# The odd middle rows of a transform: one fp32 product over 64 partitions instead of two fp32r products over 128

## The chip, the core and the metric

The kernel runs on one core of a Trainium2 chip. The metric is the device time of one execution in microseconds (us), given as the median of several runs; less is better. The engines are named as in the profile: PE is TensorE's matrix product, PEld its weight load, DVE is VectorE, ACT ScalarE, POOL GpSimd and SP the engine that issues most transfers.

## What is computed

A two-dimensional Fourier transform of eight batches of 3072 x 256 numbers, of which the real part is kept, and then a feed-forward layer with a parametric ReLU on each of the 24576 rows.

```python
X = np.fft.fft(x, axis=1)
X = np.fft.fft(X, axis=2)
x = X.real.astype(np.float32).reshape(B * S, D)      # 24576 x 256
h = x @ w_in                                         # 256 -> 2048
g = np.maximum(h, 0.0) + alpha * np.minimum(h, 0.0)
return (g @ w_out).astype(np.float32)                # 2048 -> 256
```

## The kernel before

**The feed-forward stream.** The transform along the 256 features is folded into `w_in`. What is left is the transform along the 3072 positions, batch by batch, whose result stands in the tile `X`, and the two products of the layer. They run as one stream of steps. A step takes one block of output columns (386, 384 or 512 wide) and one sixteenth of the 2048 hidden units. `ffn1` makes its two halves of the hidden product in six fp32r matmuls (`pq`, lines 755 to 757), `pair` makes sums and the ReLU of them (`d`, `pq`; DVE at 781 and 728, ACT at 785), `split_parts` cuts each into a high and a low part (`hi` on ACT at 734, `lo` on POOL at 736), and `ffn2` multiplies these with `woh` and `wol` in twelve matmuls (line 854). A step works three steps ahead on `ffn1`. The first batch has 64 steps, the six in the middle 48 each, the last 64.

**The transforms beside it.** While the steps of batch b run, batch b + 1 is folded (line 415, on POOL and DVE) and transformed. A batch has eight transforms, each one call of `dft` (line 557): the four even ones, `see`, `cee`, `ceo` and `seo`, one in each of four steps that the table `UNITS` names, between the fourth and the last pair of `ffn2`'s product groups; and two odd ones, `ca` and `sb`, for the cosine part `co` and two for the sine part `so`, in the first and the fourth step of the next batch (`unit_odd`). A transform writes one PSUM bank `ps`, which is one of the four banks that `ffn1` uses too. The order on every engine is the order of the program; there is no scheduler.

**The middle rows.** The folded rows are kept in tiles of 128 partitions, and a transform needs sums over rows with an odd index, of which 32 lie on partitions 96 to 127 of one tile and 32 on partitions 64 to 95 of another. Where `middle` holds nothing for a batch (the first two), `dft` makes the odd sum out of three fp32 matmuls of 192 to 194 columns. From the third batch on, `mids` first gathers these 64 rows: ACT writes their high part (fp32r) to partitions 64 to 127 of a tile (line 600), POOL the low part to partitions 0 to 63 (line 601). The odd sum is then two fp32r matmuls over 128 partitions, one with the high part of the table (`mh`) and one with its low part (`ml`), and one fp32 matmul. `parts_table` cuts the six tables so at six steps of the second batch. The calls `mids("se")` and `mids("ce")` stand at step 37 of a middle batch, `mids("co")` and `mids("so")` at steps 44 and 46, each of these two behind `turn_rows`, in which ACT scales six pieces (line 486) and POOL adds them (lines 488 and 489). At the end of a block, `evacuate` copies `acc` out of PSUM, half on ACT (line 891) and half on DVE.

**In the trace.** An fp32 matmul shows as two matmul records and two weight loads, an fp32r matmul as one of each. A record's shape begins with the part of the array that it uses, as rows times columns: 128\*128 everywhere, but 128\*8 in two early transforms of one feature column (tile `f`), which have 8 output partitions.

Of the kernel before, what the change touches and what calls it, by code (L numbers as in the profile page):

```python
# [9 lines left out]
F32 = mybir.dt.float32  # L10
# [80 lines left out]
def _tables():  # L91
    p = PI.reshape(3, P)
    j, i2 = J1[None, :], J2[None, :]

    def five(full, whole=False):

        n = full.shape[-1]
        at = np.concatenate([np.arange(97), [0]]) if n == 193 else np.arange(96)
        full = np.concatenate([full, np.zeros((3, P, n % 2))], 2)
        r = p[:, :, None] % 4  # L100
        if whole:
            at = np.arange(n)
        parts = [full[0][:, at] * (r[0] == 0), full[0] * (r[0] % 2), full[1][:, at] * (r[1] == 2), full[1] * (r[1] % 2)]
        return np.concatenate(parts + [full[2]], 1)

    def both(full):

        n = full.shape[-1] // 2 * 2 + full.shape[-1] % 2 * 2
        v = np.zeros((P, 194))
        rows = np.concatenate([full[1][ROW[1]], full[0][ROW[0]]])  # L110
        two = np.zeros((64, n))
        two[:, :full.shape[-1]] = rows
        v[:, :n] = np.concatenate([two, two])[:, np.arange(n).reshape(n // 2, 2).T.reshape(-1)]
        return v

    turn, q = _cos(p, 3072), p[:, :, None]
    s = _sin(q * (2 * i2 + 1), 1536)
    s[0][0] = _sin(384 * (2 * i2 + 1), 1536)[0]
    made = dict(
        cee=_cos(q * j, 768), see=_sin(q * j, 768), ceo=_cos(q * (2 * i2 + 1), 1536), seo=s,  # L120
        ca=turn[:, :, None] * _cos(q * j, 768), sb=turn[:, :, None] * _sin(q * j, 768),
    )
    m, d = np.arange(D)[:, None], np.arange(P)[None, :]
    feat = np.stack([_cos(m * d, D), _sin(m * d, D)], 1)
    feat[:, 1, 0] = (-1.0) ** np.arange(D)
    feat = feat.reshape(2, P, 2, P).transpose(1, 0, 2, 3)
    ident = np.stack([np.eye(P), -np.eye(P)], 1)
    out = dict(
        ee=np.stack([five(made["cee"]), five(made["see"])], 1), eo=np.stack([five(made["ceo"]), five(made["seo"])], 1),
        er=np.concatenate([five(made["ca"], True), five(made["sb"])], 1), mids=np.stack([both(v) for v in made.values()], 1),  # L130
        feat=feat, ident=ident,
    )
    return {k: np.ascontiguousarray(v, dtype=np.float32) for k, v in out.items()}
# [19 lines left out]
def fft2_prelu_ffn(ctx: ExitStack, tc: tile.TileContext, t, outputs):  # L153
# [367 lines left out]
    TABS = dict(cee=ee[:, 0], see=ee[:, 1], ceo=eo[:, 0], seo=eo[:, 1], ca=er[:, 0:968], sb=er[:, 968:])  # L521
    middle = {}

    def parts_table(kind):

        n, v = list(TABS).index(kind), []
        for h in "hl":
            v.append(late.tile([P, 194], F32R, tag=f"m{kind}{h}", name="m" + h))
        S.activation(out=v[0], in_=raw_mids[:, n], func=ACTF.Copy)
        G.tensor_tensor(out=v[1], in0=raw_mids[:, n], in1=v[0].bitcast(F32), op=ALU.subtract)  # L530
        middle[kind] = v

    def dft(kind, v, zr, m, mid=None, bank=None):

        ps = (bank or other_bank())[0:m]
        tab = TABS[kind]
        w, o = {778: (98, 194), 768: (96, 192), 968: (193, 194)}[tab.shape[-1]]
        col = np.cumsum([0, w, o, w, o, o])
        t_ = [tab[:, a:b] for a, b in zip(col, col[1:])]
        first, second = [(v[:, 0], t_[0])], [(v[:, 1], t_[2])]  # L540
        if zr is not None:
            r = res[:, 98:98 + 193 + (mid is not None)] if w == 193 else res[:, 0:w]
            if mid is not None:
                first.insert(0, (zr, r))
            else:
                first.append((zr.bitcast(F32), r.bitcast(F32)))
        if mid is None:
            odd = [(v[:, 0], t_[1]), (v[:, 2], t_[4]), (v[:, 1], t_[3])]
        else:
            odd = [(mid, _halves(u[:, 0:o])) for u in middle[kind]] + [(v[:, 2], t_[4])]  # L550
        sums = [(0, first), (OAT, odd), (w, second)]
        if w == 193:
            sums = [(0, first + second), (OAT, odd)]
        for at, terms in sums:
            for i, (lhsT, rhs) in enumerate(terms):
                out = ps[:, at:at + int(np.prod(rhs.shape[1:]))]
                nc.tensor.matmul(  # L557
                    out=_pairs(out) if len(rhs.shape) > 2 else out, lhsT=lhsT, rhs=rhs,
                    start=(i == 0), stop=(i == len(terms) - 1),
                )  # L560
        return ps, 192 if o == 192 else 193, m, kind
# [30 lines left out]

    def mids(b, nm):

        two = middle[nm] = late.tile([P, 2, P], F32R, tag=f"m{nm[0]}", name="m" + nm)
        v, o = fold[b, nm, "all"], 3 if nm[1] == "o" else 0
        for c in range(2):
            r = ROW[c]
            hi, lo, v2 = two[r], two[r.start - 64:r.stop - 64], v[r, o + c:o + c + 4:3]
            S.activation(out=hi, in_=v2, func=ACTF.Copy)  # L600
            G.tensor_tensor(out=lo, in0=v2, in1=hi.bitcast(F32), op=ALU.subtract)

    def mid_of(nm, i):
        return middle[nm][:, i] if nm in middle else None

    def unit_odd(b, nm):

# [289 lines left out]
    LEAD = 3  # L897
    AHEAD = 4
    SPLITS = {9: (6, 7), 10: (8, 9), 11: (10, 11), 12: (12, 13), 13: (0, 1), 14: (2, 3), 15: (4, 5)}
    TABLE_STEPS = (7, 11, 18, 22, 26, 30)  # L900
    UNITS = {53: "see", 55: "cee", 57: "ceo", 58: "seo"}, {39: "see", 40: "cee", 41: "ceo", 42: "seo"}
    FOLDS = ((0, G, 0, 0.25), (1, G, 0.25, 0.5), (3, G, 0.5, 0.75), (4, G, 0.75, 1), (2, V, 0, 0.5), (5, V, 0.5, 1))

    def step(s, between=None):
# [120 lines left out]
    for b in range(NB):  # L1025
        mine = [g for g, block in enumerate(BLOCKS) if block[0] == b]
        r_odd, r_fold, r_end = (16, 16, 50) if b == 0 else (0, 4, 36)
        beside = []
        for r in range(len(mine) * KF):
            s = mine[0] * KF + r  # L1030
            g, f = divmod(s, KF)
            kind = (UNITS[b > 0]).get(r) if b + 1 < NB else None
            if kind is None:
                step(s)
            else:
                bank = lambda: unit_mm(b + 1, kind, pq.tile([P, 512], F32, tag="pq", name="ps"))
                unit(b + 1, kind, G, step(s, bank))
            if b == 0:
                if r == 3:
                    nc.sync.dma_start(out=er, in_=t["er"])  # L1040
                if r == 9:
                    column_128_store("ceo", butterfly(*column_128_mm("ceo")))
                if r in (10, 11):
                    unit(0, ("ceo", "seo")[r - 10], G)
                if r in (12, 13):
                    if r == 13:
                        fold_128(0)
                    turn_rows(0, ("co", "so")[r - 12])
                if r == 25:
                    start.close()  # L1050
                    late = ctx.enter_context(tc.tile_pool(name="late", bufs=1))
                    raw_mids = late.tile([P, 6, 194], F32, tag="raw", name="raw_mids")
                    nc.sync.dma_start(out=raw_mids, in_=t["mids"])
            if b == 1 and r in TABLE_STEPS:
                parts_table(list(TABS)[TABLE_STEPS.index(r)])
            if f == 10:
                load_xbc(g + 1)
            q = r - r_odd
            if q in (0, 3):
                unit_odd(b, ("co", "so")[q // 3])  # L1060
            if b + 1 < NB:
                if r == r_fold:
                    fold_tiles(b + 1)
                for i, e, r0, r1 in FOLDS:
                    r0, r1 = (r_fold + round(v * (r_end - r_fold)) for v in (r0, r1))
                    if r == r0:
                        by = one_by_one if e is V else spread
                        beside.append(by(fold_whole(6 * b + 6 + i, e), r0, r1))
                for x in beside:
                    next(x, None)  # L1070
                if r == r_end + 1:
                    fold_rows(b + 1)
                    fold_128(b + 1)
                for nm, at in zip(("se", "ce", "co", "so"), (51, 52, 60, 62) if b == 0 else (37, 37, 44, 46)):
                    if r == at:
                        if nm[1] == "o":
                            turn_rows(b + 1, nm)
                        if b:
                            mids(b + 1, nm)


_INS = [
# [61 lines left out]
```

## Time and profile before

| | |
|---|---|
| median of 3 runs | 1671.02 us (1669.03 to 1671.09) |
| profiled execution | 1671.85 us, of which 1670.1 us are the span from the first to the last instruction |
| granted clock of TensorE, mean | 0.998 of full |
| busy | PE 98%, PEld 87%, DVE 91%, ACT 68%, POOL 80% |
| chain that ended last | PE 80%, DVE 8%, POOL 5%, ACT 4% |

The span and 1.75 us around it make up the profiled execution, which is 0.8 us over the median. A matmul's listed duration is from its start until its last result is out; the next one starts before that, so what a matmul costs is the distance from its start to the next start.

### The profile page before, as it was taken

To read this page: it belongs to the slowest core of one execution; us is meant where nothing else is said; L and a number is where in the kernel's file an instruction comes from. 1 tells how busy PE (TensorE), PEld (TensorE's weight loads), DVE (VectorE), ACT (ScalarE), POOL (GpSimd) and SP (SyncE) were. 2 spreads that over 40 slices of the span, in tenths; PEclk is the share of its full clock that TensorE was granted. 3 is DMA by queue.
4 is the path that set the end of the run, shared out by engine and by line. 5 is a ranking of instruction groups with operands and counts; after the bars stand their busy time and mean duration, and the time that the engine had idled before them with its cause. 6 is when DMAs were issued, how large, how long until landed. Compare 5 with 4: busy or idle time off the path is not lost.

```text
span 1670.1 us, 26532 instructions
## 1 busy us (share of the span) xinstructions
PE 1639.2 (98%) x8240; PEld 1458.9 (87%) x8240; DVE 1518.1 (91%) x2708; ACT 1130.5 (68%) x2092; POOL 1341.1 (80%) x1439
## 2 busy tenths in 40 slices
PE   8989999999999999999999999999999999999998
PEld 7779999888888888888888888888888888889998
DVE  7979998999889998899989998899988999889997
ACT  5865667666676666766676666766667666677765
POOL 2378987899888887889888898888887888776666
PEclk9999999999999999999999999999999999999999
DMA  6410120011000110000100101001110010000000
GB/s 234 140 58 33 45 69 20 8 70 39 32 26 20 57 52 20 32 39 32 70 1 32 51 33 58 26 7 70 39 32 26 20 45 31 1 31 25 25 20 20
DMA packets 25403, 70.48 MB, mean 42 GB/s; under 512 B 5718, under 2 KB 7726, under 8 KB 25262
## 3 DMA queue, kind: packets, MB, share of 16 engines
q1 hardware_dynamic: 23918, 68.27, 11.5%
q8 instruction: 66, 1.08, 0.3%
q10 hardware_dynamic: 1344, 0.52, 0.1%
q14 instruction: 75, 0.61, 0.1%
HBM read 43.50 MB, written 25.26 MB: 41 GB/s over the span
## 4 chain that ended last, share of the span: by engine, by line
PE 80%; DVE 8%; POOL 5%; ACT 4%; issue 2%; DMA 1%; DVEq 0%; ACTq 0%; POOLq 0%; SPq 0%
PE acc L854 49%; PE pq L755 9%; PE pq L756 8%; PE pq L757 8%; PE ps L557 3%; DVE d L781 2%; POOL lo L736 2%; DVE d L728 2%; PE acc L824 2%; DVE pf L773 1%; ACT pq L785 1%; ACT hi L734 1%; DVE y L590 1%; DMA feat<-in_feat 1%; PE ps L351 1%
## 5 line engine op out<-in xcount | busy, mean ns | idle before, releaser
L736 POOL TENSOR_TENSOR lo<-d,hi 128x512 fp32r<-128x512 f32 (+2 forms) x804 | 971.6, 1225 | 228.5 <-ACT hi L734 205.9
L734 ACT ACTIVATE hi<-d 128x512 fp32r<-128x512 f32 (+2 forms) x804 | 482.1, 600 | 352.3 <-DVE d L728 250.0
L728 DVE SCALAR_TENSOR_TENSOR d<-d,sg,pq 128x512 f32<-128x512 f32 (+2 forms) x804 | 565.0, 703 | 22.0 <-ACT pq L785 22.0
L785 ACT ACTIVATE pq<-d,sga 128x512 f32<-128x512 f32 (+2 forms) x804 | 525.9, 655 | 54.0 <-DVE d L781 53.6
L781 DVE TENSOR_TENSOR d<-pf,pq 128x512 f32<-128x512 f32 (+2 forms) x832 | 530.4, 641 | 20.6 <-POOL lo L736 11.8
L854 PE MATMUL acc<-hi,woh 128*128 128x512 f32 (+2 forms) x1604 | 456.1, 365 | 6.4 <-ACT o L891 6.4
L854 PE MATMUL acc<-lo,woh 128*128 128x512 f32 (+2 forms) x1604 | 394.3, 366 | 0.0
L854 PE MATMUL acc<-hi,wol 128*128 128x512 f32 (+2 forms) x1604 | 392.6, 365 | 0.0
L773 DVE SCALAR_TENSOR_TENSOR pf<-xbc,w,pq 128x512 f32<-128x512 f32 (+2 forms) x416 | 298.5, 718 | 67.9 <-PE pq L757 60.5
L854 PEld LDWEIGHTS acc<-hi,woh 128*128 128x128 f32 x1604 | 297.9, 189 | 41.3 <-ACT o L891 10.5
L755 PE MATMUL pq<-X,wih 128*128 128x512 f32 (+2 forms) x832 | 310.8, 374 | 15.7 <-DVE d L728 12.2
L854 PEld LDWEIGHTS acc<-hi,wol 128*128 128x128 f32 x1604 | 295.2, 189 | 30.7
L854 PEld LDWEIGHTS acc<-lo,woh 128*128 128x128 f32 x1604 | 292.6, 189 | 29.5
L756 PE MATMUL pq<-X,wih 128*128 128x512 f32 (+2 forms) x832 | 302.5, 364 | 0.3 <-DVE X L661 0.3
L757 PE MATMUL pq<-X,wil 128*128 128x512 f32 (+2 forms) x832 | 302.4, 363 | 0.0
L755 PEld LDWEIGHTS pq<-X,wih 128*128 128x128 f32 x832 | 157.2, 189 | 48.5 <-PE pq L757 12.0
L757 PEld LDWEIGHTS pq<-X,wil 128*128 128x128 f32 x832 | 157.6, 189 | 15.5
L756 PEld LDWEIGHTS pq<-X,wih 128*128 128x128 f32 x832 | 157.7, 190 | 14.5 <-issue 0.5
L415 POOL TENSOR_TENSOR raw<-raw 128x512 f32<-128x512 f32 (+2 forms) x84 | 69.5, 827 | 0.0
L320 POOL TENSOR_TENSOR w<-we,wm 128x512 int32<-128x512 int32 x16 | 20.4, 1272 | 44.4 <-DVE wm L311 43.3
L891 ACT ACTIVATE o<-acc 128x512 f32<-128x512 f32 (+2 forms) x50 | 25.6, 563 | 22.4 <-PE acc L854 22.2
L661 POOL TENSOR_TENSOR X<-yo,X 128x384 fp32r<-128x384 f32 x32 | 31.1, 993 | 11.2 <-ACT X L660 11.2
(184 smaller groups left out, 1099.2 us busy)
## 6 DMA issues: line engine op xcount, KB each, us to landing
raw<-in_xh SPq DMA_DIRECT2D x46, 512.0 KB
out<-o SPq DMA_DIRECT2D x36, 512.0 KB
raw<-in_w SPq DMA_DIRECT2D x15, 512.0 KB
xbc<-xcd SPq DMA_DIRECT2D x18, 256.0 KB
out<-o SPq DMA_DIRECT2D x8, 386.0 KB
out<-o SPq DMA_DIRECT2D x6, 384.0 KB
before<-in_xh SPq DMA_DIRECT2D x2, 512.0 KB
xbc<-xcd SPq DMA_DIRECT2D x5, 193.0 KB
```

The lines of the kernel that those rows point to most:

```text
L415: yield size, lambda o=o, i0=i0, i1=i1, op=op: e.tensor_tensor(out=o, in0=i0, in1=i1, op=op)
L557: nc.tensor.matmul(out=_pairs(out) if len(rhs.shape) > 2 else out, lhsT=lhsT, rhs=rhs, start=(i == 0), stop=(i == len(terms) - 1),)
L728: V.scalar_tensor_tensor(out=g, in0=d, scalar=sg[:, f:f + 1], in1=ad, op0=ALU.mult, op1=ALU.max)
L734: S.activation(out=hi, in_=d, func=ACTF.Copy)
L736: G.tensor_tensor(out=lo, in0=d, in1=hi.bitcast(F32), op=ALU.subtract)
L755: nc.tensor.matmul(out=out, lhsT=wih[:, f, q], rhs=xh, start=True, stop=False)
L756: nc.tensor.matmul(out=out, lhsT=wih[:, f, q], rhs=xl, start=False, stop=False)
L757: nc.tensor.matmul(out=out, lhsT=wil[:, f, q], rhs=xh, start=False, stop=True)
L773: V.scalar_tensor_tensor(out=_pairs(pf), in0=_halves(xbc[g]), scalar=w128[:, f:f + 1], in1=_pairs(ps[0]), op0=ALU.mult, op1=ALU.add,)
L781: V.tensor_tensor(out=d, in0=pf, in1=ps[1], op=ALU.add if i else ALU.subtract)
L785: S.activation(out=ad, in_=d, func=ACTF.Copy, scale=sga[:, f:f + 1])
L854: nc.tensor.matmul(out=out, lhsT=wt[:, f, o * P:(o + 1) * P], rhs=rhs, start=(f == 0 and n[o] == 0), stop=(f == KF - 1 and n[o] == 2),)
```

## The change

Six things change.

- `mids` copies the 64 rows once, in fp32, to partitions 64 to 127. The two subtractions on POOL are gone.
- The odd sum's two fp32r products become one fp32 product whose two operands lie on partitions 64 to 127 alone.
- `parts_table` with its six ACT copies and six POOL subtractions is gone; the table is loaded to 64 partitions and used as it is.
- The second batch, too, gets gathered rows: its `mids` calls run at steps 51, 52, 60 and 62 of the first batch. Its transforms have two fp32 products in the odd sum instead of three.
- With that, the small product with `zres` in `cee` and `ca` of the second batch is fp32r instead of fp32, as it was from the third batch on.
- `see` and `cee` move from steps 39 and 40 to steps 38 and 39.

```diff
     def both(full):
-        n = full.shape[-1] // 2 * 2 + full.shape[-1] % 2 * 2
-        v = np.zeros((P, 194))
...
+        v = np.zeros((64, 194))
+        v[:, :full.shape[-1]] = np.concatenate([full[1][ROW[1]], full[0][ROW[0]]])
...
-            odd = [(mid, _halves(u[:, 0:o])) for u in middle[kind]] + [(v[:, 2], t_[4])]
+            odd = [(mid, mids_of[64:, list(TABS).index(kind), 0:o]), (v[:, 2], t_[4])]
...
-        two = middle[nm] = late.tile([P, 2, P], F32R, tag=f"m{nm[0]}", name="m" + nm)
+        two = middle[nm] = late.tile([P, 2, P], F32, tag=f"m{nm[0]}", name="m" + nm)
         v, o = fold[b, nm, "all"], 3 if nm[1] == "o" else 0
         for c in range(2):
-            r = ROW[c]
-            hi, lo, v2 = two[r], two[r.start - 64:r.stop - 64], v[r, o + c:o + c + 4:3]
-            S.activation(out=hi, in_=v2, func=ACTF.Copy)
-            G.tensor_tensor(out=lo, in0=v2, in1=hi.bitcast(F32), op=ALU.subtract)
+            S.activation(out=two[ROW[c]], in_=v[ROW[c], o + c:o + c + 4:3], func=ACTF.Copy)

     def mid_of(nm, i):
-        return middle[nm][:, i] if nm in middle else None
+        return middle[nm][64:, i] if nm in middle else None
...
-    UNITS = {53: "see", 55: "cee", 57: "ceo", 58: "seo"}, {39: "see", 40: "cee", 41: "ceo", 42: "seo"}
+    UNITS = {53: "see", 55: "cee", 57: "ceo", 58: "seo"}, {38: "see", 39: "cee", 41: "ceo", 42: "seo"}
...
-            if b == 1 and r in TABLE_STEPS:
-                parts_table(list(TABS)[TABLE_STEPS.index(r)])
...
-                        if b:
-                            mids(b + 1, nm)
+                        mids(b + 1, nm)
```

On PE, the transform `see` of the third batch, between two groups of `ffn2`'s products, reads so before (`mh` and `ml` are the table's parts, `mse` the gathered rows, `ee` the large table, `fse` the folded rows):

```order
L854 MATMUL acc<-hi,woh 128x512 x2
L557 MATMUL ps<-ee,fse 128x98
L557 MATMUL ps<-mh,mse 128x194
L557 MATMUL ps<-ml,mse 128x194
L557 MATMUL ps<-ee,fse 128x194
L557 MATMUL ps<-ee,fse 128x98
L854 MATMUL acc<-lo,woh 128x512 x4
```

and so now:

```order
L838 MATMUL acc<-hi,woh 128x512 x2
L544 MATMUL ps<-ee,fse 128x98
L544 MATMUL ps<-mids_of,mse 128x194
L544 MATMUL ps<-ee,fse 128x194
L544 MATMUL ps<-ee,fse 128x98
L838 MATMUL acc<-lo,woh 128x512 x4
```

One matmul stands where two stood, in fp32 and on 64 partitions of its operands; the program has 56 of them, eight for each batch from the second on.

On POOL, around step 37 of the second batch, the order before is (the `lo` rows are the stream's, `X<-y` is the store of a transform's low part):

```order
L736 TENSOR_TENSOR lo<-d,hi 128x512 x4
L476 CAST zres<-zst 33x384
L460 COPY fso<-f_142 128x6
L462 CAST zres<-r_97 1x1 x2
L601 TENSOR_TENSOR mse<-fse,mse 32x256 x2
L601 TENSOR_TENSOR mce<-fce,mce 32x256 x2
L736 TENSOR_TENSOR lo<-d,hi 128x512 x5
L661 TENSOR_TENSOR X<-y,X 128x385
```

and now:

```order
L720 TENSOR_TENSOR lo<-d,hi 128x512 x4
L472 CAST zres<-zst 33x384
L456 COPY fso<-f_142 128x6
L458 CAST zres<-r_97 1x1 x2
L720 TENSOR_TENSOR lo<-d,hi 128x512 x3
L645 TENSOR_TENSOR X<-y,X 128x385
```

The four subtractions are gone from between the casts and the stream's `lo`, and the first store of a transform comes two `lo` (one step) earlier.

On ACT, at the end of the first batch (`part` is `turn_rows`, `o<-acc` the copy out of PSUM), before:

```order
L486 ACTIVATE part<-fso,inputs 128x128 x6
L891 ACTIVATE o<-acc 128x384 x2
L734 ACTIVATE hi<-d 128x512
L785 ACTIVATE pq<-d,sga 128x512
L734 ACTIVATE hi<-d 128x512
```

and now:

```order
L482 ACTIVATE part<-fso,inputs 128x128 x6
L585 ACTIVATE mso<-fso 32x256 x2
L875 ACTIVATE o<-acc 128x384 x2
L718 ACTIVATE hi<-d 128x512
L769 ACTIVATE pq<-d,sga 128x512
```

Two copies of gathered rows, which read what POOL adds in `turn_rows`, now stand ahead of the copies out of PSUM there, as they already did in the later batches.

## Rows read from the trace of the kernel before

**Rows 1.** The page, part 1: busy time, share and instructions of each engine.

```profile
PE 1639.2 (98%) x8240; PEld 1458.9 (87%) x8240; DVE 1518.1 (91%) x2708; ACT 1130.5 (68%) x2092; POOL 1341.1 (80%) x1439
```

**Rows 2.** The waits of PE over the span: us, times, longest.

```profile
PE pq L755 <- DVE d L728: 12.2, 26, 1.9
```

**Rows 3.** Timeline of PE, `see` of the third batch: start us, listed duration us.

```profile
441.81 0.36 PE L557 MATMUL ps<-ee,fse 128*128 128x98 f32 x2
...
442.73 1.11 PE L854 MATMUL acc<-lo,woh 128*128 128x512 f32 x4
...
444.19 0.38 PE L757 MATMUL pq<-X,wil 128*128 128x512 f32 x1
444.85 0.48 PE L755 MATMUL pq<-X,wih 128*128 128x512 f32 x1 [0.28 <-DVE d L728]
```

**Rows 4.** Timeline of PE, `see` of the second batch, and four of its passes.

```profile
243.68 1.57 PE L557 MATMUL ps<-ee,fse 128*128 128x98 f32 x10
245.03 0.57 PE L854 MATMUL acc<-lo,woh 128*128 128x384 f32 x2
...
244.24 0.82 PE L557 MATMUL ps<-ee,fse 128*128 128x194 f32 x4
```

**Rows 5.** Timelines of PE and PEld, into and out of a 128\*8 transform.

```profile
87.64 0.28 PE L351 MATMUL ps<-w,feat 128*128 128x128 f32 x1
87.84 0.25 PE L557 MATMUL ps<-eo,f 128*8 128x96 f32 x1
...
89.06 0.25 PE L557 MATMUL ps<-eo,f 128*8 128x96 f32 x1
89.24 0.43 PE L755 MATMUL pq<-X,wih 128*128 128x386 f32 x1
89.51 0.33 PE L756 MATMUL pq<-X,wih 128*128 128x386 f32 x1
...
89.24 0.19 PEld L755 LDWEIGHTS pq<-X,wih 128*128 128x128 f32 x1 [0.17 <-issue]
```

**Rows 6.** Timeline of PE, the same places around a 128\*128 transform.

```profile
93.70 0.28 PE L351 MATMUL ps<-w,feat 128*128 128x128 f32 x1
93.81 0.36 PE L557 MATMUL ps<-eo,fce 128*128 128x96 f32 x2
...
95.09 0.28 PE L557 MATMUL ps<-eo,fce 128*128 128x96 f32 x1
...
95.40 0.33 PE L756 MATMUL pq<-X,wih 128*128 128x386 f32 x1
```

**Rows 7.** Timelines of POOL and DVE after step 37 of the second batch.

```profile
437.68 1.52 POOL L601 TENSOR_TENSOR mse<-fse,mse 32x256 fp32r<-32x256 f32 x2
...
442.19 0.69 DVE L781 TENSOR_TENSOR d<-pf,pq 128x512 f32<-128x512 f32 x1 [1.13 <-POOL lo L736]
```

**Rows 8.** Timelines of POOL, DVE and PE after step 44 of the second batch.

```profile
471.54 1.52 POOL L601 TENSOR_TENSOR mco<-fco,mco 32x256 fp32r<-32x256 f32 x2 [0.52 <-ACT mco L600]
...
474.46 0.69 DVE L781 TENSOR_TENSOR d<-pf,pq 128x512 f32<-128x512 f32 x1 [0.54 <-POOL lo L736]
...
475.10 0.38 PE L757 MATMUL pq<-X,wil 128*128 128x512 f32 x1
475.95 0.45 PE L755 MATMUL pq<-X,wih 128*128 128x512 f32 x1 [0.47 <-DVE d L728]
```

**Rows 9.** Timelines of ACT and PE, the end of the second batch's last block.

```profile
480.19 0.85 ACT L600 ACTIVATE mso<-fso 32x256 fp32r<-32x256 f32 x2 [1.21 <-POOL fso L489]
...
481.71 0.97 PE L854 MATMUL acc<-hi,woh 128*128 128x512 f32 x2 [0.99 <-ACT o L891]
```

**Rows 10.** Timelines of ACT, POOL and PE, the end of the first batch.

```profile
280.59 0.84 ACT L891 ACTIVATE o<-acc 128x384 f32<-128x384 f32 x2
...
280.86 1.01 POOL L489 TENSOR_TENSOR fso<-fso,part 128x384 f32<-128x384 f32 x1
...
281.78 0.59 PE L854 MATMUL acc<-hi,woh 128*128 128x512 f32 x2
```

More of the change, by code (lines that the diff above doesn't have):

```diff
@@ L106, in both @@
     def both(full):
-        n = full.shape[-1] // 2 * 2 + full.shape[-1] % 2 * 2
-        v = np.zeros((P, 194))
[L110 to L113, printed above, removed]
+        v = np.zeros((64, 194))
+        v[:, :full.shape[-1]] = np.concatenate([full[1][ROW[1]], full[0][ROW[0]]])
         return v
@@ L522, in fft2_prelu_ffn @@
     middle = {}
[L524 to L531, printed above, removed]
     def dft(kind, v, zr, m, mid=None, bank=None):
@@ L899, in fft2_prelu_ffn @@
     SPLITS = {9: (6, 7), 10: (8, 9), 11: (10, 11), 12: (12, 13), 13: (0, 1), 14: (2, 3), 15: (4, 5)}
-    TABLE_STEPS = (7, 11, 18, 22, 26, 30)
-    UNITS = {53: "see", 55: "cee", 57: "ceo", 58: "seo"}, {39: "see", 40: "cee", 41: "ceo", 42: "seo"}
+    UNITS = {53: "see", 55: "cee", 57: "ceo", 58: "seo"}, {38: "see", 39: "cee", 41: "ceo", 42: "seo"}
     FOLDS = ((0, G, 0, 0.25), (1, G, 0.25, 0.5), (3, G, 0.5, 0.75), (4, G, 0.75, 1), (2, V, 0, 0.5), (5, V, 0.5, 1))
@@ L1051, in fft2_prelu_ffn @@
                     late = ctx.enter_context(tc.tile_pool(name="late", bufs=1))
-                    raw_mids = late.tile([P, 6, 194], F32, tag="raw", name="raw_mids")
-                    nc.sync.dma_start(out=raw_mids, in_=t["mids"])
-            if b == 1 and r in TABLE_STEPS:
-                parts_table(list(TABS)[TABLE_STEPS.index(r)])
+                    mids_of = late.tile([P, 6, 194], F32, name="mids_of")
+                    nc.sync.dma_start(out=mids_of[64:], in_=t["mids"])
             if f == 10:
```

## The prediction

> **What bounds the kernel now.** I read the busy table first: PE is busy 98% of the span [rows 1]. The listed lengths of matmuls overlap, so I then read the timeline of PE by starts: inside the stream the passes follow each other without a gap, and the kernel is as long as PE's passes plus the places where PE waits. The waits of PE say how much there is to get back: 12.2 us in all for sums by DVE (`d`, L728), in 26 places [rows 2]. So an edit counts in three ways only: the time that PE's own passes take, these waits, and new waits. GpSimd's load as such is no bound; it matters where its queue makes DVE late. POOL's and DVE's timelines are for that.
>
> **PE's passes, without regard to array shape.** `see` of the third batch, with one fp32r pair and one fp32 matmul of 194 columns in its odd sum, takes 442.73 - 441.81 = 0.92 us [rows 3]. `see` of the second batch, with three fp32 matmuls there, takes 245.03 - 243.68 = 1.35 us [rows 4]. One fp32 matmul is two passes of 0.163 us (four passes listed as 0.82, less the listed length of the last, 0.33 as for the other pass of that many cycles in rows 6, over three distances) [rows 4, 6], so 0.33 us. The new transform has two fp32 matmuls: 1.35 - 0.33 = 1.02 us. That is 0.10 us dearer than the fp32r pair, in 48 transforms (eight in each of six batches): **+4.8 us**. In the second batch each of eight transforms loses one fp32 matmul: **-2.6 us**. The `zres` product there goes from fp32 to fp32r in three transforms, which is worth less than two passes in each and is left out of the sum.
>
> **PE's passes, with regard to array shape.** This is the term that decides. Each of the 56 new matmuls uses 64 of the array's rows, and its neighbours on both sides use 128. The trace before has no matmul on 64 rows. It does have matmuls on another part of the array than 128\*128, the two 128\*8 transforms, so I read what happens on the way into one and out of it, beside the same places at an ordinary transform.
>
> - Out of it: from the start of the last 96-column pass to the start of the second pass behind it, 89.51 - 89.06 = 0.45 us, against 95.40 - 95.09 = 0.31 us. The load of the next weights was idle for 0.17 us with nothing to wait for ("issue"); it begins 0.18 us after the last narrow pass, instead of running beneath it [rows 5, 6]. Price 0.14 us.
> - Into it: 87.84 - 87.64 = 0.20 us from the last wide pass to the first narrow one, against 93.81 - 93.70 = 0.11 us. Price 0.09 us, though the load is only 8 columns [rows 5, 6].
>
> So a change of shape makes the next weight load wait until the pass before it is through. **Low bound of the price** of one matmul between two changes: 0.23 us, the row as it is. But the new loads are 128 columns wide, and 128-column passes follow each other at 0.11 us [rows 6], which bounds a bare load. In: 0.09 + 0.11 = 0.20 us. Out, behind a 194-column pass under which the next load is hidden today: the wait of 0.10 us (0.18 us less the 0.08 us that 96 columns take, half of 0.163) and a bare load of 0.11 us, 0.21 us. Together 0.41 us if both loads lie bare. I take **0.36 us**, near that end because all loads here are of full width, and under it because around the 98-column passes PE is bound by loads already. 56 x 0.36 = **+20.2 us**. The least bound is zero (a 64-row pass between 128-row passes needs no such wait); the most is that the load waits for the full listed length of the pass (0.25 us for 96 columns, 0.33 us for the wider one [rows 5, 6]) and then takes 0.11 us: 0.25 + 0.11 - 0.11 in and 0.33 + 0.11 - 0.16 out, 0.53 us.
>
> The Trainium skill has a rule on this (TensorEngine Tiling (Array Packing), Key Properties): "Changing tiling mode (not just tile) drains the TensorE". By that rule the 64-row matmuls pay on both sides; it has no price for the drain, and the rows give the one used above. The trace agrees for 128\*8; no row of it shows 64 rows. The rule taken away, the sum below would be 20.2 us lower.
>
> **GpSimd's subtractions.** At step 37 POOL makes four of them, 1.52 us for the first two and as much for the others, before it can go on with the stream's `lo`. DVE then sits idle 1.13 us for `lo` [rows 7], and PE's next product starts 444.85 - 444.19 = 0.66 us after the one before, where 0.22 us is the rule between 512-column passes (0.44 us lost) [rows 3]. At step 44 there are two: DVE idle 0.54 us, PE 475.95 - 475.10 = 0.85 us, 0.63 us lost [rows 8]. With the subtractions gone I count both as gained: 1.07 us in six batches, **-6.4 us**. Their cover otherwise is complete: the six of `parts_table` lie between the folds, and no wait of PE is near them. ACT's copies stay, and the copies at step 46 wait 1.21 us for POOL's additions of `turn_rows` (L489), not for the subtractions; the copy out of PSUM stands behind them, and PE waits 0.99 us for it [rows 9]. That is not removed. The waits for `d` left in rows 2 lie partly in the steps with odd transforms; there a longer transform gives DVE time. I allow **-1.5 us**. Moving `see` and `cee` a step forward shifts the same work; `see` then stands right behind the four copies on ACT (two pairs like that of 0.85 us in rows 9), but POOL has two times 1.52 us less [rows 7]. I cost it at nothing; without that cover it would cost what step 37 costs now, 0.44 us in six batches, 2.6 us.
>
> **New waits.** At the end of the first batch ACT today copies `acc` at 280.59, and PE needs the bank at 281.78. Now two copies of 0.85 us together [rows 9] come before it, and they wait for POOL's L489, which ends at 280.86 + 1.01 = 281.87 [rows 10]. The first half of the copy is then through at 281.87 + 0.85 + 0.42 = 283.14, so PE waits about 1.4 us, and some 0.4 us for the second half (two passes listed as 0.97 us where PE had to wait, 0.59 us where it had not [rows 9, 10]). The pair at step 60 holds ACT in the same way; I add 0.7 us, half of what it holds. **+2.5 us**, once.
>
> **The sum.** 4.8 - 2.6 + 20.2 - 6.4 - 1.5 + 2.5 = +17.0 us on a profiled execution of 1671.85 us: 1688.9 us. That execution is 0.8 us over the median, so 1688 us against 1671.02.
>
> **The rivals.**
>
> - *No price for 64 rows.* What speaks for it: nothing in the trace changes rows, only output columns; the rows that are used keep their places. The sum loses 20.2 us: 1668 us, on the edge of faster and no change. This is the other side, and the price from which it decides is easy to give: at 0.06 us per matmul (3.3 us over 56) gain and loss cancel, and above 0.12 us the kernel is measurably slower. Chance 0.15.
> - *The price is that of the 128\*8 rows*, 0.23 us or a little less, since the next load can partly run ahead: 56 x 0.23 = 12.9 us, 1681 us. Chance 0.15.
> - *The whole pass must be through*, 0.53 us: 29.7 us, 1697 us. For it: the idle 0.17 us ends before the listed end of the pass (89.06 + 0.25 = 89.31, the load starts at 89.24 [rows 5]), which speaks against. Chance 0.08.
> - *The change does not free the waits*, because ACT's copies, which stay, hold `hi` and with it `lo`: 6.4 us are not gained, 1694 us. Against it: at step 37 ACT was through at once and POOL was late by itself [rows 7]. Chance 0.07.
> - The forecast, 1688 us: 0.55.
>
> **How the numbers follow.** The kernel's runs lie within 0.2% (3.3 us), about what a measurement can tell from no change. The first rival's 1668 us lies on that edge, so I split it: faster 0.08, same 0.08. All others are slower: 0.84. The range leaves out most of the first rival and the far end of the third: 1671 to 1697.
>
> **What would show it.** The pass of `mids_of` should show as two 64-row passes, with an idle time of PEld before the first and before the load behind the second, and about 0.28 us from the pass before to the first, 0.36 us from the second to the next; `see` of the third batch should take about 1.38 us instead of 0.92. POOL should go from the casts straight to `lo`, and PE should not wait at steps 38 and 45. At the end of the first batch PE should wait for `o` for over a microsecond. The prediction is wrong if passes of 64 rows follow those of 128 at 0.11 to 0.16 us; then `see` takes 1.02 us and the kernel 1668.

## The result: 1686.5 us, 0.97% slower

The changed kernel takes 1686.51 us (median of 4 runs, 1685.73 to 1688.79), the kernel before 1671.05 us. The ratio is 1.0097, with a 95% interval of 1.008 to 1.0115. The forecast was 1688 us. The profiled execution after, 1688.79 us, has a span of 1687.0 us; 1.9 us of its distance to the one before lie ahead of the first batch's odd transforms, at 125.85 us instead of 123.94, where the two programs are the same (the mean granted clock of TensorE was 0.95 in the first 125 us, and 0.97 in the first 123 us before; it stood at 0.50, its lower level of 1.2 GHz, from 30.6 to 37.2 us and from 119.3 to 125.9 us, after PE had been busy 25.3 of 29 us and 76.5 of 81.4 us at 2.4 GHz), so that 15 us are left to explain. One execution of an experiment's kernel, at 3506.27 us about twice its others, is left out of that kernel's median.

The page after, part 1 (answers to [rows 1]):

```profile
PE 1660.4 (98%) x8221; PEld 1467.1 (87%) x8221; DVE 1517.9 (90%) x2708; ACT 1134.4 (67%) x2094; POOL 1303.8 (77%) x1385
```

POOL lost 37 us of work, and the kernel is slower: PE is busy 21.2 us longer than in [rows 1], about as much as the 15 us and the recovered waits together.

Timelines of PE and PEld after, `see` of the third batch (answers to [rows 3]):

```profile
442.82 0.36 PE L544 MATMUL ps<-ee,fse 128*128 128x98 f32 x2
443.11 0.59 PE L544 MATMUL ps<-mids_of,mse 64*128 64x194 f32 x2
443.63 0.79 PE L544 MATMUL ps<-ee,fse 128*128 128x194 f32 x4
444.20 0.46 PE L838 MATMUL acc<-lo,woh 128*128 128x512 f32 x1
...
442.82 0.19 PEld L544 LDWEIGHTS ps<-ee,fse 128*128 128x128 f32 x1
443.11 0.29 PEld L544 LDWEIGHTS ps<-mids_of,mse 64*128 64x128 f32 x2
443.63 0.63 PEld L544 LDWEIGHTS ps<-ee,fse 128*128 128x128 f32 x4 [0.23 <-issue]
```

The transform takes 444.20 - 442.82 = 1.38 us, where it took 0.92 us. The two passes of `mids_of` show as 64\*128. The load behind them was idle for 0.23 us with nothing to wait for ("issue") and starts together with its pass, at 443.63, instead of beneath the pass before it. So did the first load of the two, at 443.11: the pass before it started at 442.90, and the load before it was through at 442.82 + 0.19 = 443.01, so this one was idle for 0.10 us, which the view does not mark.

The waits of PE over the span, after (answers to [rows 2]):

```profile
PE pq L739 <- DVE d L712: 8.0, 17, 1.9
PE acc L838 <- ACT o L875: 7.7, 7, 1.5
```

The waits for DVE's sums fell from 12.2 to 8.0 us and from 26 to 17. Behind steps 37 and 44 there is none left: in the timeline of PE from 436 to 490 us the only one is at the end of the block.

```profile
487.16 0.97 PE L838 MATMUL acc<-hi,woh 128*128 128x512 f32 x2 [0.98 <-ACT o L875]
```

That is the wait of [rows 9], untouched. One like it is new at the end of the first batch (timelines of ACT and PE, answer to [rows 10]):

```profile
285.22 0.84 ACT L585 ACTIVATE mso<-fso 32x256 f32<-32x256 f32 x2 [1.21 <-POOL fso L485]
286.08 0.87 ACT L875 ACTIVATE o<-acc 128x384 f32<-128x384 f32 x2
...
280.99 0.45 PE L739 MATMUL pq<-X,wih 128*128 128x512 f32 x1 [0.43 <-DVE d L712]
286.63 0.86 PE L838 MATMUL acc<-hi,woh 128*128 128x512 f32 x2 [1.38 <-ACT o L875]
```

The copies wait for POOL, the copy out of PSUM waits behind them, and PE waits for that.

### The profile page after: what moved, and what is told of

Its sections match the earlier page's. It is cut to its first block, busy times and chain, and to the rows that moved or that the text cites. A ratio compares the mean times of both kernels' runs of the same rounds, so it can differ in the third digit from the quotient of the medians.

```text
span 1687.0 us, 26445 instructions
## 1 busy us (share of the span) xinstructions
PE 1660.4 (98%) x8221; PEld 1467.1 (87%) x8221; DVE 1517.9 (90%) x2708; ACT 1134.4 (67%) x2094; POOL 1303.8 (77%) x1385
## 5 line engine op out<-in xcount | busy, mean ns | idle before, releaser
L739 PEld LDWEIGHTS pq<-X,wih 128*128 128x128 f32 x832 | 157.8, 190 | 35.2 <-PE pq L741 7.3
L875 ACT ACTIVATE o<-acc 128x512 f32<-128x512 f32 (+2 forms) x50 | 25.6, 564 | 22.8 <-PE acc L838 22.6
L645 POOL TENSOR_TENSOR X<-yo,X 128x384 fp32r<-128x384 f32 x32 | 31.1, 993 | 10.5 <-ACT X L644 10.5
```

What stands on the lines that cost most here:

```text
L645: lo_engine.tensor_tensor(out=lo, in0=v, in1=hi.bitcast(F32), op=ALU.subtract)
L739: nc.tensor.matmul(out=out, lhsT=wih[:, f, q], rhs=xh, start=True, stop=False)
```

## The experiments

The theory: each 64-row product among 128-row passes costs PE about 0.37 us, because the weight loads at its two edges cannot run ahead; the waits that GpSimd caused did go. The rivals: the product is dear in itself (fp32, or the second batch's new rows), or the freed GpSimd time brought nothing. Every ratio is to the kernel before, timed on the same chip.

**Zeros on the other 64 partitions.** The table gets 64 rows of zeros on top, the gathered rows a tile whose lower half is written with zeros once. The arithmetic is the same and every pass is 128\*128.

```diff
-            odd = [(mid, mids_of[64:, list(TABS).index(kind), 0:o]), (v[:, 2], t_[4])]
+            odd = [(mid, mids_of[:, list(TABS).index(kind), 0:o]), (v[:, 2], t_[4])]
...
+                    for k in "cs":
+                        gathered[k] = late.tile([P, 2, P], F32, name="m" + k)
+                        G.memset(gathered[k][0:64], 0.0)
```

> The changed kernel, but the gathered rows and their table lie on 128 partitions with zeros on the lower 64, so that the one fp32 product has the shape of its neighbours. Same arithmetic, no change of array shape. Theory (a change of the array's rows costs about 0.37 us for each of the 56 products): 20.7 us less than the changed kernel's 1686.5, so 1666 us, below the kernel before. Rival (the fp32 product itself or the second batch's gathered rows cost the time): 1684 to 1688 us.

Measured: 1669.37 us, ratio 0.9984 (0.9975 to 0.9993). That is 3 us more than the 1666 expected: the kernel before took 1672.07 us on this chip, 1 us more than in the result, and part of the rest is in the short waits below. Still, the 64-row product alone turns a small gain into a loss. Timelines of PE and PEld of this kernel, the same transform and then the first odd pair of the third batch:

```profile
438.00 0.36 PE L544 MATMUL ps<-ee,fse 128*128 128x98 f32 x2
438.20 0.52 PE L544 MATMUL ps<-mids_of,ms 128*128 128x194 f32 x2
438.55 0.69 PE L544 MATMUL ps<-ee,fse 128*128 128x194 f32 x4
439.02 0.46 PE L838 MATMUL acc<-lo,woh 128*128 128x512 f32 x1
...
438.11 0.30 PEld L544 LDWEIGHTS ps<-mids_of,ms 128*128 128x128 f32 x2
438.39 0.68 PEld L544 LDWEIGHTS ps<-ee,fse 128*128 128x128 f32 x4
...
483.87 0.26 PE L544 MATMUL ps<-res,zres 128*128 128x194 f32 x1
...
486.31 0.46 PE L739 MATMUL pq<-X,wih 128*128 128x512 f32 x1
```

`see` takes 439.02 - 438.00 = 1.02 us, the time that the prediction gave it without a change of shape, and 0.36 us less than with one. Each load starts before the pass that it serves, 438.11 for 438.20 and 438.39 for 438.55. The odd pair takes 486.31 - 483.87 = 2.44 us. From `see` of the third batch to that of the fourth (635.91 - 438.00) it is 197.91 us against 200.64 us in the changed kernel (643.46 - 442.82). Eight times 0.37 us would be 3.0 us; 0.2 us of it came back as waits, all under 0.2 us each.

**Two 64-row products side by side.** In each pair of odd transforms the 64-row product goes last in `ca` and first in `sb`, so that nothing of 128 rows stands between them.

```diff
+            if kind == "ca":
+                odd.reverse()
...
+        elif kind == "sb" and mid is not None:
+            sums = [(OAT, odd), (0, first), (w, second)]
```

> The changed kernel, but in each pair of odd transforms the 64-row product comes last in the first transform and first in the second, so that 28 of the 56 products stand in 14 pairs with no 128-row pass between them. Theory (the price is paid at the changes of shape): 14 times 0.37 us less, 5.2 us, so 1681 us. Rival (each 64-row product is slow by itself, wherever it stands): no difference, 1686.5 us.

Measured: 1681.71 us, ratio 1.006 (1.0047 to 1.0073). Timelines of PE and PEld of this kernel, the pair for `co` in the third batch:

```profile
490.07 0.26 PE L548 MATMUL ps<-res,zres 128*128 128x194 f32 x1
490.17 1.16 PE L548 MATMUL ps<-er,fco 128*128 128x193 f32 x6
491.26 0.92 PE L548 MATMUL ps<-mids_of,mco 64*128 64x194 f32 x4
492.11 1.02 PE L548 MATMUL ps<-er,fco 128*128 128x194 f32 x6
492.91 0.46 PE L743 MATMUL pq<-X,wih 128*128 128x512 f32 x1
...
491.26 0.62 PEld L548 LDWEIGHTS ps<-mids_of,mco 64*128 64x128 f32 x4 [0.23 <-issue]
492.11 0.19 PEld L548 LDWEIGHTS ps<-er,fco 128*128 128x128 f32 x1 [0.23 <-issue]
```

Four 64-row passes, one idle time of the load before them and one behind. The pair takes 492.91 - 490.07 = 2.84 us; in the changed kernel it takes 493.33 - 490.13 = 3.20 us.

```profile
490.13 0.26 PE L544 MATMUL ps<-res,zres 128*128 128x194 f32 x1
...
493.33 0.46 PE L739 MATMUL pq<-X,wih 128*128 128x512 f32 x1
```

One change in and out saved is 0.36 us, 14 of them 5.1 us. So the price stands at the change, not at the product.

**The second batch as before.**

```diff
-                        mids(b + 1, nm)
+                        if b:
+                            mids(b + 1, nm)
```

> The changed kernel, but the second batch again gets no gathered rows: its odd sums are three fp32 products, and ScalarE makes no copies at the end of the first batch. Theory: the new waits there (2.5 us) go, the passes there cost the same within 0.3 us, so 1684 us. Rival (the second batch gains what its third fp32 product cost, 2.6 us): 1689 us.

Measured: 1683.61 us, ratio 1.0069 (1.0056 to 1.0083). In the traces the way from `see` of the second batch to that of the third is 194.25 us (437.18 - 242.93) against 197.11 us (442.82 - 245.71): 2.9 us. The second batch's rows were a loss: its passes gain next to nothing (0.2 us over its transforms), since the change of shape eats the third fp32 product, and ScalarE's copies stand ahead of the copy out of PSUM.

**The kernel before without GpSimd's low parts.** The low parts of the gathered rows stay at the zeros that are written once.

```diff
-            G.tensor_tensor(out=lo, in0=v2, in1=hi.bitcast(F32), op=ALU.subtract)
```

> The kernel before, with the subtractions of the gathered rows on GpSimd left out: the low parts are zeros written once, so their share of the result is missing; TensorE's products and ScalarE's copies stay as they are. Theory: the waits behind steps 37 and 44 go, 1.1 us a batch, with some of the others, 6.4 to 8 us in all, so 1663 to 1665 us. Rival (ScalarE's copies hold the chain, so nothing comes free): 1671 us.

Measured: 1665.55 us, ratio 0.9964 (0.9952 to 0.9977), 6.0 us less by the ratio, with an interval of 3.8 to 8.0. From `see` to `see` it is 197.26 us (642.81 - 445.55) against 198.59 us (640.40 - 441.81), 1.3 us a batch. The waits behind steps 37 and 44 are gone, and those for DVE's sums fell from 12.2 us in 26 places [rows 2] to 9.0 us in 14; the one at the end of the block is as it was.

```profile
PE pq L753 <- DVE d L726: 9.0, 14, 1.9
```

**The late copies.** Since the wait at the end of each block is as large as those that went, two kernels move the gathering for the odd transforms one step later, behind the copy out of PSUM: one on the kernel with zeros, one on the kernel before, which keeps its fp32r pairs.

```diff
-                    if r == at:
-                        if nm[1] == "o":
-                            turn_rows(b + 1, nm)
+                    if r == at and nm[1] == "o":
+                        turn_rows(b + 1, nm)
+                    if r == at + (nm[1] == "o"):
                         mids(b + 1, nm)
```

> The kernel with zeros on the lower 64 partitions, and the copies of the gathered rows for the two odd transforms one step later (behind the copies out of PSUM at the end of a block, instead of ahead of them). Theory (ScalarE's copies, which wait there for GpSimd, hold the copy out of PSUM): the 1.4 us at the end of each of six batches and about 2.6 us at the end of the first go, 11 us, so 1656 to 1659 us. Rival (the wait moves to the next place where ScalarE is late): at most 3 us, 1664 to 1667 us.

> The kernel before with only the gathering for the two odd transforms one step later, copies on ScalarE and subtractions on GpSimd alike. Theory: the 1.4 us at the end of each of six batches and the 0.6 us behind step 44 go, 10 to 12 us if the subtractions do no harm at the new places, so 1659 to 1661 us. Rival (the subtractions make the stream's low parts late there as they did before): 1664 to 1668 us.

Measured: 1652.26 us, ratio 0.9891 (0.9876 to 0.9906), and 1653.31 us, ratio 0.9896 (0.9883 to 0.991). Both gain more than was expected. Timeline of ACT in the first, the end of the second batch:

```profile
470.72 1.84 ACT L482 ACTIVATE part<-fso,inputs 128x128 f32<-128x128 f32 x6
472.47 1.05 ACT L875 ACTIVATE o<-acc 128x512 f32<-128x512 f32 x2
...
475.78 0.84 ACT L585 ACTIVATE ms<-fso 32x256 f32<-32x256 f32 x2
```

ACT goes from its pieces straight to the copy out of PSUM, and no wait for POOL precedes the copies any more. On the kernel with zeros a batch takes 196.04 us instead of 197.91 us, 1.9 us less, where 1.4 us were expected from the wait named; the way from the second batch to the third (433.31 - 241.58 = 191.73 us instead of 194.67 us) and the way from the last `see` to the end (235.9 us instead of 239.1) gained more than was worked out. By the starts of PE's passes 1.5 of the 1.9 us are the wait at the end of the block and what follows it, and the rest are waits under 0.1 us beside it. At the end of the first batch, between 260 and 300 us, PE's waits for DVE's sums fell as well, from 0.7 to 0.2 us, and between the last `see` and 1500 us from 1.0 to 0.5 us. On the kernel before, the wait behind step 37 stays and the one behind step 44 goes with the others, 2.7 us a batch.

**The steps of `see` and `cee`.** On the kernel before, alone:

```diff
-    UNITS = ..., {39: "see", 40: "cee", 41: "ceo", 42: "seo"}
+    UNITS = ..., {38: "see", 39: "cee", 41: "ceo", 42: "seo"}
```

> The kernel before with only the table of steps changed: see and cee at steps 38 and 39 instead of 39 and 40. Theory (the move shifts the same work): within 1 us of the kernel before, 1671 us; at worst the wait of step 37 grows, which would be up to 3 us more. Rival (the move is part of what took the waits away): 2 to 3 us less.

Measured: 1674.13 us, ratio 1.0018 (1.0009 to 1.0027). Timeline of PE of this kernel:

```profile
437.89 0.36 PE L557 MATMUL ps<-ee,fse 128*128 128x98 f32 x2
439.20 0.35 PE L557 MATMUL ps<-mh,mse 128*128 128x194 f32 x1 [0.94 <-POOL mse L601]
```

`see` comes before GpSimd has its low parts, and PE waits for them itself: 1.31 us from the first start to that of `mh`, where 0.14 us is the rule, so 1.2 us in place of the 0.44 us that it lost behind step 37 before. By the ratio the kernel is 3 us slower, the worst case of the expectation and not the 1 us of its theory. And undone in the changed kernel:

> The changed kernel with see and cee back at steps 39 and 40. Theory (without the subtractions on GpSimd the place of the two transforms costs nothing): within 1 us of the changed kernel, 1686 us. Rival (the move by itself costs what it cost in the kernel before, 3 us): 1683 us.

Measured: 1687.24 us, ratio 1.0096 (1.008 to 1.0113), no difference from the changed kernel. Without the subtractions the move is free.

**The changed kernel again**, on the chip of the late copies:

> The changed kernel once more, unedited, on the same chip as the three others. Theory: 15 to 16 us over the kernel before, as in the result, and 19 to 21 us over the kernel with zeros on the lower 64 partitions.

Measured: 1685.8 us, ratio 1.0094 (1.008 to 1.0107). The kernel with zeros stands at 0.9984 of the kernel before, so the distance is 1.1% or 18 us, a little under the 19 to 21 us expected; the short waits that came back are part of the rest.

**Late copies and `ce` at step 38.** On the kernel before with late copies, the four subtractions are spread over two steps.

```diff
-                ... if b == 0 else (37, 37, 44, 46)):
+                ... if b == 0 else (37, 38, 44, 46)):
```

> The kernel before with the gathering for the odd transforms one step later, and that for cee and ceo at step 38 instead of 37, so that GpSimd makes two subtractions in a step instead of four. Theory (the wait behind step 37 comes from four subtractions in a row): 0.44 us less in each of six batches than with the late copies alone, 2.6 us, so 1650 to 1651 us. Rival (the two later ones make the low parts late at step 38 instead): 1653 us, no difference.

Measured: 1649.11 us, ratio 0.9872 (0.9856 to 0.9889), the fastest here and 1 us under the expectation. Timeline of POOL:

```profile
436.08 1.53 POOL L601 TENSOR_TENSOR mse<-fse,mse 32x256 fp32r<-32x256 f32 x2
437.69 2.52 POOL L736 TENSOR_TENSOR lo<-d,hi 128x512 fp32r<-128x512 f32 x2
440.29 1.52 POOL L601 TENSOR_TENSOR mce<-fce,mce 32x256 fp32r<-32x256 f32 x2
```

The stream's `lo` stands between the two pairs, and by the starts of its passes no wait of PE over 0.2 us is left between 300 and 660 us. A batch takes 195.2 us instead of 198.6.

## Why the prediction was right, step by step

- **The price of the shape**, 0.36 us taken between bounds of 0.23 and 0.41: `see` with and without it differ by 0.36 us (1.38 and 1.02), the odd pairs by 3.20 - 2.44 = 0.76 us, 0.38 us each. For 56 products that is 20.6 us; 20.2 us were forecast. The reading of [rows 5] that carried it held: the load waits until the pass before it is through, and then lies bare, beneath no pass. That its width of 128 columns makes the difference to the 0.23 us of the 128\*8 rows fits the distances, but no run varies the width. One detail fell differently. The prediction expected 0.28 us from the pass before to the first 64-row pass and 0.36 us from the second to the next. A bare load's pass is listed from the load's start, so the trace shows only 443.11 - 442.90 = 0.21 us and 443.63 - 443.38 = 0.25 us there, and the load's time in the distance behind each, 0.27 us both times; with zeros the four are 0.11, 0.16, 0.19 and 0.16 us. So about half of the price is waiting and half is load, and the sum over the transform is the one forecast. That the price belongs to the change is shown by the products side by side; that it does not belong to fp32 is shown by the zeros. Whether 64 rows on partitions 0 to 63, or an fp32r product, would cost the same no run here shows.
- **The fp32 product for the fp32r pair**, 0.10 us in 48 transforms: 1.02 against 0.92 us, and 2.44 against 2.23 us for two. It held.
- **The second batch**, -2.6 us for its third product and +0.36 us eight times: `see` there takes 1.38 us (247.09 - 245.71) instead of 1.35. It held. The `zres` products that were left out of the sum are the rest: the pairs of odd transforms there fell from 3.31 to 3.20 us.
- **GpSimd's subtractions**, 6.4 us and 1.5 us of other waits: 6.0 us by the ratio of the kernel without them, 1.3 us a batch by its trace, which is 7.9 us in six. It held, and the rival that ScalarE's copies hold the chain fell. In the changed kernel the batches grew by 2.05 us while PE's passes grew by 3.80 us (four even transforms by 0.46 to 0.47 us, two odd pairs by 0.97 us each), so 1.75 us of waits went per batch, 0.4 us more than the kernel without low parts got back. That belongs to the longer transforms. Behind the first odd pair PE's second group of products starts 487.91 - 487.45 = 0.46 us after the pass before it in the kernel before, and as late without the low parts (490.32 - 489.86), but after 494.06 - 493.84 = 0.22 us, the rule, in the changed kernel; with zeros, whose transforms are longer by 0.8 us a batch, 1.5 us of waits went. The prediction allowed 1.5 us in all for this and the other waits, and counted too little.
- **The new waits**, 2.5 us once: 2.9 us by the traces of the kernel that undoes them.
- **The earlier steps**, costed at nothing, and at 2.6 us without cover: nothing in the changed kernel, 3 us (0.9 to 2.7 thousandths) in the kernel before. It held, though by another wait than was named: PE stood for the low parts themselves.

The terms together: about 22.6 us of longer passes where 22.4 were forecast, 2.9 us of new waits where 2.5 were, and some 10.5 us of waits gone (six times 1.75) where 7.9 were. They add up to the 15 us that were left to explain, against 17.0 forecast. The one term that was sized too small is that of the waits; the other two misses run against it, so the total is a little closer than its parts, which is luck.

The rival on the other side, no price for 64 rows, named 1668 us; the kernel with zeros, which is that case, measured 1669.37.

## What to carry to other kernels

On an engine that is the bound, a matmul on half of the rows is not a saving: between full-shape passes it cost 0.36 us here, more than its own two passes of 0.16 us each, and filling the unused rows with zeros was faster with the same result. If products of another shape are needed, put them next to each other, since the price is paid at the change. And before an engine's load is cut, ask which of its instructions stand ahead of something that the bound waits for: two pairs of copies of 0.85 us in each batch, moved behind a copy out of PSUM and so away from additions that they had to wait for, were worth 16 to 17 us in the whole kernel, while some 36 us of GpSimd work (24 pairs of 1.52 us) were worth 6.

## What had not been expected of the hardware

The Trainium skill says that changing the tiling mode drains TensorE (TensorEngine Tiling (Array Packing), Key Properties). The trace agrees in that the next weight load waits, for a change of rows as for one of columns: PEld is idle for 0.23 us behind a 194-column pass of 64 rows, 0.17 us behind a 96-column pass of 8 columns. It does not show a wait for the pass's listed end: the load starts at 443.63, and the two 64-row passes are listed until 443.11 + 0.59 = 443.70. Within the 64-row passes loads run ahead as usual: the four passes of the pair side by side are listed as 0.92 us together.

What was not expected is how much the start of one program differs between executions: `see` of the second batch begins at 243.68 us in the profile of before and at 247.42 us in that of the same kernel without low parts, though nothing differs ahead of it but two small writes of zeros. Most of it goes with the granted clock of TensorE. Stretches of before (the first) and of the kernel without low parts (the other two), with the busy time of PE, PEld, DVE, ACT and POOL and then the granted clock:

```profile
119.80:123.00 3.20, 3.18 (x10) 3.20 (x11) 3.20 (x7) 3.01 (x8) 3.20 (x5) 0.50 0.62 248
119.30:125.90 6.60, 6.06 (x19) 6.09 (x20) 5.43 (x11) 5.28 (x12) 6.60 (x9) 0.50 0.30 121
190.90:194.20 3.30, 3.22 (x10) 3.25 (x11) 3.30 (x7) 2.00 (x5) 2.39 (x3) 0.50 0.00 0
```

The clock stands at its lower level, 1.2 of 2.4 GHz, for 3.2 us in one execution and for 9.9 us in the other; a stretch of 3.2 us at 31 us is the same in both. Ahead of the fall at 119 us PE was busy 35.2 of 39 us in both; ahead of the one at 190.9 us it was busy 61.1 of 64.5 us, and in the kernel before, where no such fall came, 65.0 of 66.7 us. The 6.7 us more at half the clock make 3.4 of the 3.7 us. Differences of single executions under some 4 us are therefore read from `see` to `see`, not from the span.
